# Attention and gated MLP on one core: the order of the first QKV tiles, two buffers and two kinds of adds changed

## The chip, the cores and the metric

The kernel runs on one core of a Trainium2 chip. The metric is the device time of one execution in microseconds (us); lower is better. The engines are named as the profile names them: PE (TensorE; PEld is its weight load), DVE (VectorE), ACT (ScalarE), POOL (GpSimd), SP (SyncE, which here only starts transfers). A name with a q (ACTq, POOLq, SPq) is the engine's DMA queue.

## The reference, cut to what matters

One layer in fp32 with S=2048 tokens and D=576 channels; the MLP has F=4608 hidden channels.

```python
q, k, v = heads_of(layernorm(x) @ wqkv)         # 32 heads of 18
# token s attends to s, s-2, ..., s-14 (W=8, dilation 2, none below 0)
logits = einsum("bhsd,bhswd->bhsw", q, kg) * Dh ** -0.5
o = einsum("bhsw,bhswd->bhsd", softmax(logits + mask), vg)
h = x + o @ wo
n = layernorm(h)
out = h + (sigmoid(n @ w_gate) * (n @ w_up)) @ w_down
```

## The kernel before, in words

**Tiles.** Tokens are split by parity (the dilation is 2) and by half into four blocks of 512 (`BLOCKS`, b = 0 to 3), each of four tiles of 128 (`NS`, index j). The 32 heads form four groups of eight (`NG`, index g).

**Products.** An fp32 product is made of three matmuls. `split` (L103 to L105) writes the high part with an ACT copy and the low part with a DVE subtraction; the products are high by high, low by high and high by low. So each operand of PE costs one pass of ACT and then one of DVE. The hidden size is cut into 36 pieces f of 128. For most of them two blocks are multiplied together by seven products of sums and differences instead of eight, and `sums` and `operands` make those sums.

**The attention stage**, the first 240 us or so:

- `ln1` (L327 on) norms a block. `ln_j` does one tile: statistics on DVE, a power on POOL, and then either DVE (L134, L135) or ACT (L130 to L132, with `on_act`) writes the normed tile. Before the change, ACT does it for blocks 2 and 3. PE transposes the tile (`tr_main`, L139, and `tr_rest`), and `split` makes `th` and `tl` of it.
- `qkv(b, g)` multiplies the four tiles of a block by the weights of one group (`tok_major`, L146 to L153). ACT evicts each product (L361). Behind the fourth eviction ACT's queue takes three transfers that write q (L363) and k and v (L366) to DRAM.
- `attention(b, g)` loads these rows through SP, multiplies and reduces them on DVE (L172, L175, L180 to L189, L198 to L206), with the softmax exponential on ACT (L185). For block 0 the result stays in SBUF; otherwise it is spilled to DRAM by POOL's queue (L209, L211).
- `att_all` holds the order of the attention work: (b, g) = (0,0), (0,1), (1,0), (0,2), (0,3), (1,1), (1,2), (1,3). It is interleaved by hand with the QKV work: `heads` runs `qkv` for a list of (b, g) and advances the attention by `step(ag, n)` after each tile, and `norm` does so between normed tiles. The groups of blocks 2 and 3 are attended later, under the MLP.
- `front` makes block 0's output projection, residual and second norm as soon as its four groups are attended.

**The MLP** runs over a list of pieces: 14 plain pieces for block 0 alone (`single`), 22 pieces for blocks 0 and 1 together (`pair`), 14 plain pieces for block 1 alone, and 36 pieces for blocks 2 and 3 together. Two pieces make a segment of the down product. In the plain pieces `down_std` makes a segment's four tiles (PE, L661) and adds them up in one SBUF tile called `stage`: the first of the seven segments by an ACT copy (L669), the other six by a DVE add (L671). Behind the seventh, `add_dram` (L677) adds the tile to DRAM through POOL's queue. The pool of `stage` tiles has two buffers. The pair segments go through ACT and `add_dram` in any case.

**Work under the MLP.** While PE multiplies, a background generator goes on with the rest: block 1's last attention, then for blocks 1 to 3 `proj_scr` (load of the spilled attention result `oj`, transposes, output projection, second norm), then `operands`, which makes the operands of the paired products. `proj_scr` copies its normed and transposed tiles to SBUF (`raw`) or, where `raw` is None, writes them tile by tile to DRAM (`xj`, `xscr`), from which `operands` loads them again as `ar`. Before the change, block 3 takes the way through DRAM: its operand sums (L260 to L270, in `sums`) wait for that load.

**The tail.** `load_tails` (L1021 to L1039) fetches the partial results of blocks 2 and 3 from DRAM into tiles `tail` and `more`, and three DVE adds (L1038) put them together under the last pieces. In the same pieces `pair` has three DVE adds of its own, L623, L636 and L641, which PE's next products wait for.

**What sets the order.** Each engine runs its instructions in a fixed order. A list scheduler writes that order from the program: it takes the ready instruction of the highest priority, `tc.high_priority(n)` raises the priority (HI = 400, HC = 700), and `tc.issue_after(x)` holds an instruction behind another one. A buffer of a pool is free again when its last reader is done.

Of the kernel before, what the change touches and what calls it, by code (L numbers as in the profile page):

```python
# [15 lines left out]
F32 = mybir.dt.float32  # L16
# [5 lines left out]
P = 128  # L22
S = 2048
D = 576
# [31 lines left out]
NPL = 4  # L56
LAG = 3


@with_exitstack  # L60
def kernel(ctx, tc, x, wqkv, wo, wmlp, out):
# [32 lines left out]
    hsev = dr.tile([P, 2, 7, 2, DH2], F32, name="h7")  # L94
    xscr = [dr.tile([P, 5, TB], F32, name=f"x{b}") for b in range(4)]
    wscr = [dr.tile([P, 2, 5, DH2], F32, name=f"wo{i}") for i in range(2)]
# [229 lines left out]
    def ln1(b, xb):  # L326
        th = th3_tile(F32R) if b == 3 else th_tile()  # L327
        tl = tl_tile()
        yield th, tl
        xn = tok_tile()  # L330
        for j in range(NS):
            js = slice(j * P, (j + 1) * P)
            pri = 2 * HI if b == 0 else HI if b > 1 else 0
            with tc.high_priority(pri):
                ln_j(xb[:, j], xn[:, j], b > 1)
            pv = tr_main(mm_tile(), xn[:, j])
            pr = tr_rest(acc_tile(), xn[:, j])
            with tc.high_priority(pri):
                split(th[:, 0:4, js], tl[:, :, js], pv)
                split_rest(th[:, 4, js], pr)  # L340
            yield
# [93 lines left out]
    wos = [None, wo_w(1, swo.tile([P, 2, 5, DH2], F32R, tag="wo", name="wo1"))]  # L435
    heads(((1, 2), (0, 3), (2, 2), (3, 2)), w, 2)
    wos[0] = wo_w(0, saw.tile([P, 2, 5, DH2], F32R, tag="qw", bufs=2, name="wow"))
# [151 lines left out]
    def single(X, w, t, units, side):  # L589
# [21 lines left out]
        return {t: hid}  # L611

    def pair(X, w, between, last):
        b1, b2, b3 = b_tile(0), b_tile(1), b_tile(2)
# [7 lines left out]
        with tc.high_priority(HC):  # L622
            dve.tensor_tensor(s1, s1, b2, ALU.add)  # L623
            act.activation(s1, s1, AF.Sigmoid)
# [9 lines left out]
        with tc.high_priority(HC):  # L634
            act.activation(s3, b1, AF.Copy)
            dve.tensor_tensor(s3, s3, b3, ALU.add)  # L636
        between(4)
        prod(b3, X["a11"], w, "t4", False)
        rest(b3, X["a11"], w, "g4")
        with tc.high_priority(HC):  # L640
            dve.tensor_tensor(s2, s2, b3, ALU.add)  # L641
            act.activation(s2, s2, AF.Sigmoid)
# [45 lines left out]
    def down_std(seg, b, n):  # L688
        if n == 0:
            tails[b] = st.tile([P, NS, D], F32, name="stage")  # L690
        hs = tails[b]
        for j in range(NS):
            add_tile(halved(hs, j), down_tile(seg, b, j), n == 0)
            if j == NS - 1 and n == NSTD // 2 - 1:
                add_dram(b, hs)
            yield
# [59 lines left out]
    def proj_scr(pj, b, raw, wos, ins=None, after=None):  # L756
# [3 lines left out]
        def tile_j(t, j):  # L760
            js = slice(j * P, (j + 1) * P)
            xj = []

            def put(pv, cs):
                if cs.start == 0:
                    if b < 2:
                        pool.dma_start(hacc[b][:, j], t[1])
                    else:
                        rows = slice(0, 7, 6) if b == 2 else slice(2, 5, 2)
                        pool.dma_start(hsev[:, j // 2, rows, j % 2],  # L770
                                       t[1].rearrange("p (i n) -> p i n", i=2))
                    if raw is None:
                        xj.append(pj.tile([P, 5, P], F32, bufs=2, name="xj"))
                act.activation(xj[0][:, cs] if raw is None else raw[:, cs, js], pv, AF.Copy)

            yield from proj_j(bg_bank, t, wos, th[:, :, js], tl[:, :, js], lambda: t[0], put, (1, 0))
            if raw is None:
                act.dma_start(xscr[b][:, :, js], xj[0])

# [25 lines left out]
        for j, gn in enumerate(live):  # L805
            yield from gn
            if after is not None:
                nxt.append([load_j(pj, after, j, i) for i in range(2)])
        if raw is not None:
            act.dma_start(xscr[b][:, 0:2], raw[:, 0:2])  # L810
        return nxt

    def operands(pp, p, Xn, names, own):
        def load(t):
            a = pp.tile([P, 5, TB], F32, name=f"ar{t}")
            pool.dma_start(a, xscr[2 * p + t])
            return a

        a0 = load(0) if p == 0 else own
        a1 = load(1) if p == 1 else own  # L820
        s = [pp.tile([P, 2, TB], F32, name=f"rs{i}") for i in range(3)]
# [14 lines left out]
    def under_first():  # L836
        wos = [None, wos_early()]
        for _ in ag:
            yield ATT
        at_stk.close()  # L840
        a1 = xt.tile([P, 5, TB], F32, tag="th", bufs=3, name="ar")
        with sb_pool("pj", "right") as pj:
            while c < 5:
                yield
            yield from proj_scr(pj, 1, a1, wos)
        with sb_pool("pp", "right") as pp:
            yield from operands(pp, 0, X, ("s2", "s3", "s1", "a11", "s4"), a1)

# [4 lines left out]
    def under_rest(last_x):  # L853
# [14 lines left out]
        with sb_pool("pj2", "right") as pj:  # L868
            a0 = xt.tile([P, 5, TB], F32, tag="th", bufs=3, name="ar")
            ins = yield from proj_scr(pj, 2, a0, wos, after=3)  # L870
            yield from proj_scr(pj, 3, None, wos, ins)
        z = st.tile([P, NS, D], F32, name="stage")
        pool.memset(z, 0.0)
        for u in range(2):
            act.dma_start(hsev[:, u, 1:6:2], z[:, 0:3].rearrange("p k (i n) -> p k i n", i=2))
        pp = pp_stk.enter_context(sb_pool("pp2", "right"))
        raw = yield from operands(pp, 1, Xn, ("s2", "s3", "s4"), a0)
        yield raw
# [142 lines left out]
    def load_tails():  # L1021
# [15 lines left out]
        for a, m in adds:  # L1037
            dve.tensor_tensor(a, a, m, ALU.add)  # L1038
            yield  # L1039
# [124 lines left out]
```

## Time and profile before

| | |
|---|---|
| time, three runs | 1611.44, 1617.32, 1623.48 us |
| median | 1617.32 us |
| profiled execution: time | 1618.58 us |
| profiled execution: span | 1616.8 us |
| mean granted PE clock in it | 0.991 |
| instructions in the span | 22443 |
| HBM read, written | 147.19 MB, 130.35 MB (172 GB/s over the span) |

The profile is one profiled execution, so its rows are to be set against its own 1618.58 us. On the page, part 1 gives the busy time of each engine with its share of the span; the parts after it are the span in 40 slices, the DMA queues, the chain of work that ended last, the costliest groups of instructions and the DMA issues. In a row for a group, "out<-in" are the tiles' names, "x4" the count, "3.0, 768" the busy time in us and the mean of one in ns, and what follows the last bar is the idle time of the engine ahead of them with the work that ended it. In a timeline a row begins with the start in us and the duration in us, and what stands in brackets at its end is the wait ahead of it. In a table of stretches each engine has its busy time and the number of its instructions, followed by the clock granted to PE.

### The profile page before, as it was taken

What the parts mean: (1) busy time and instruction counts of PE and PEld (TensorE: products, weight loads), DVE (VectorE), ACT (ScalarE), POOL (GpSimd) and SP (SyncE); (2) the same over time, 40 slices, a digit from 0 to 9 for tenths busy, and PEclk for the clock granted to TensorE, in tenths of its full rate; (3) what the DMA queues carried; (4) which work ended last, traced back from release to release, by engine and by line L of the source; (5) the groups of instructions that cost most, each with busy time, mean ns of one, the idle gap of its engine ahead of it and who ended that gap; (6) DMA issues with size and microseconds to landing.
All of it is one profiled execution on the core that took longest, in us unless ns stands there. A gap on an engine that the chain in (4) does not pass through costs nothing.

```text
span 1616.8 us, 22443 instructions
## 1 busy us (share of the span) xinstructions
PE 1570.3 (97%) x8532; PEld 1387.0 (86%) x8532; DVE 1277.2 (79%) x2002; ACT 877.2 (54%) x1537; POOL 184.8 (11%) x227
## 2 busy tenths in 40 slices
PE   7899889999999999999999999999999999999997
PEld 6899878887888888888898978888888888888887
DVE  7998898968999999999555668776677776677655
ACT  4423235434555566556434335776677776677651
POOL 2000010010001000000110100112112112112110
PEclk9999999999999999999999999999999999999999
DMA  7446555354367665675874435788888888888882
GB/s 246 177 149 225 216 180 183 113 196 173 103 161 192 167 152 154 157 197 141 252 230 153 136 109 150 154 167 181 171 169 189 174 168 181 169 172 189 170 185 94
DMA packets 79612, 276.65 MB, mean 171 GB/s; under 512 B 8368, under 2 KB 16816, under 8 KB 78480
## 3 DMA queue, kind: packets, MB, share of 16 engines
q0 software_dynamic: 28000, 107.79, 34.4%
q1 hardware_dynamic: 40304, 143.70, 27.3%
q10 hardware_dynamic: 11200, 23.73, 3.9%
q8 instruction: 67, 1.10, 0.3%
q14 instruction: 41, 0.34, 0.1%
HBM read 147.19 MB, written 130.35 MB: 172 GB/s over the span
## 4 chain that ended last, share of the span: by engine, by line
PE 64%; issue 17%; DVE 8%; DMA 6%; POOL 4%; ACT 1%; SPq 0%; POOLq 0%; ACTq 0%; DVEq 0%
PE b L554 30%; PE dp L661 13%; PE acc L150 6%; PE dp L723 6%; PE b L561 5%; POOL h L732 3%; DMA wg<-in_wmlp_dram 2%; DVE lg L175 1%; DVE w L105 1%; DVE pr L172 1%; DVE pr L198 1%; PE bgp L150 1%; PE b L150 1%; DMA o<-kw 1%; DMA kw<-k 1%
## 5 line engine op out<-in xcount | busy, mean ns | idle before, releaser
L554 PE MATMUL b<-tl,w 128*128 128x512 f32 x1728 | 446.6, 398 | 7.8 <-ACT s L628 4.1
L554 PEld LDWEIGHTS b<-tl,w 128*128 128x128 f32 x1728 | 313.8, 190 | 69.1 <-ACT s L628 5.4
L554 PE MATMUL b<-th,w 128*128 128x512 f32 x1380 | 359.6, 395 | 2.3 <-DVE s L574 2.3
L554 PEld LDWEIGHTS b<-th,w 128*128 128x128 f32 x1380 | 251.8, 189 | 56.4 <-DVE s L636 4.0
L561 PE MATMUL b<-th,w 128*128 128x512 f32 x576 | 178.0, 391 | 0.0
L104 ACT ACTIVATE w<-wg 128x384 fp32r<-128x384 f32 (+2 forms) x200 | 117.8, 595 | 106.8 <-DMA wg<-in_wmlp_dram 46.1
L729 ACT ACTIVATE ev<-dp 128x576 f32<-128x576 f32 x224 | 145.0, 648 | 33.2 <-PE dp L723 30.5
L732 POOL DMA_DIRECT2D h<-ev x128 | 109.8, 858 | 457.0 <-ACT ev L729 449.6
L105 DVE TENSOR_TENSOR w<-wg,w 128x384 fp32r<-128x384 f32 (+2 forms) x200 | 128.5, 648 | 39.0 <-ACT w L104 38.8
L150 PE MATMUL acc<-qw,th 128*128 128x432 f32 x512 | 156.8, 367 | 0.0
L105 DVE TENSOR_TENSOR w<-tw,w 128x512 fp32r<-128x512 f32 x116 | 79.6, 686 | 70.9 <-ACT w L104 70.3
L561 PEld LDWEIGHTS b<-th,w 128*128 128x128 f32 x576 | 108.6, 189 | 23.3
L661 PE MATMUL dp<-d,h1h 128*128 128x288 f32 x640 | 119.8, 296 | 2.4 <-ACT h1h L104 2.4
L104 ACT ACTIVATE w<-tw 128x512 fp32r<-128x512 f32 x116 | 73.3, 632 | 87.0 <-PE b L554 79.2
L661 PE MATMUL dp<-d,h0h 128*128 128x288 f32 x640 | 118.7, 295 | 1.0 <-ACT h0h L104 1.0
L661 PEld LDWEIGHTS dp<-d,h0h 128*128 128x128 f32 x640 | 99.6, 189 | 5.2 <-ACT h0h L104 1.2
L661 PEld LDWEIGHTS dp<-d,h1h 128*128 128x128 f32 x640 | 98.8, 189 | 5.6 <-ACT h1h L104 2.8
L150 PEld LDWEIGHTS acc<-qw,th 128*128 128x128 f32 x512 | 98.8, 193 | 4.8 <-ACT th L104 0.3
L150 PE MATMUL acc<-qw,tl 128*128 128x432 f32 x256 | 93.8, 367 | 0.0
L361 ACT ACTIVATE ev<-acc 128x432 f32<-128x432 f32 x64 | 33.9, 529 | 108.1 <-PE acc L153 107.7
L172 DVE TENSOR_TENSOR pr<-kw,q 128x1152 f32<-128x1152 f32 x64 | 85.2, 1353 | 7.9 <-DMA kw<-k 7.3
L669 ACT ACTIVATE stage<-dp 128x576 f32<-128x576 f32 x96 | 62.2, 648 | 53.3 <-PE dp L661 42.4
(270 smaller groups left out, 2898.8 us busy)
## 6 DMA issues: line engine op xcount, KB each, us to landing
h<-ev POOLq DMA_DIRECT2D x96, 576.0 KB, 6.8
wg<-in_wmlp_dram SPq DMA_DIRECT2D x49, 928.0 KB, 5.4
h<-stage POOLq DMA_DIRECT2D x24, 1152.0 KB, 11.7
wg<-in_wmlp_dram SPq DMA_DIRECT2D x36, 640.0 KB, 4.9
kw<-k SPq DMA_DIRECT2D x16, 792.0 KB, 4.7
vw<-v SPq DMA_DIRECT2D x16, 792.0 KB, 6.4
wd<-in_wmlp_dram SPq DMA_DIRECT2D x18, 576.0 KB, 6.7
h<-ev POOLq DMA_DIRECT2D x32, 288.0 KB, 6.1
```

What stands on the lines that cost most here:

```text
L104: act.activation(hi, src, AF.Copy)
L105: splits.append(dve.tensor_tensor(lo, src, f32(hi), ALU.subtract))
L150: pe.matmul(ps[:, :n], a[:, c, js], m[:, c], start=k == 0, stop=False)
L172: dve.tensor_tensor(pr[:, i], kw[:, j:j + W], q[:, j].unsqueeze(1).broadcast_to([P, W, CG]), ALU.mult)
L361: act.activation(ev[:, :, j], ps[:, :NQ].rearrange("p (t c) -> p t c", t=3), AF.Copy)
L554: pe.matmul(ps, wt[:, a, k0 + c], xx[:, m + c], start=first and k == 0, stop=k == 5, skip_group_check=True)
L561: pe.matmul(ps, wt[:, a, k0], xx[:, 4], start=False, stop=a == 1, skip_group_check=True)
L661: pe.matmul(ps[:, i, :DH2], a[:, js], d[:, m, i * DH2:(i + 1) * DH2], start=k == 0, stop=k == n)
L669: act.activation(hv, ps, AF.Copy)
L723: pe.matmul(ps[:, i, :DH2], a[x][:, js], m[y], start=k in (0, 1, 3) and q == 0, stop=q == 2, skip_group_check=True)
L729: act.activation(hs[:, k % 2], ps[:, :, :DH2], AF.Copy)
L732: pool.dma_start(hsev[:, u, k0:k + 1], hs[:, :k + 1 - k0], accum_op=ALU.add, max_dma_last_dim=8 * D)
```

## The change

Five things are changed.

1. The order of the QKV work: after the first two tiles of (1,2) come the four tiles of (0,3) and then the other two tiles of (1,2). Before, (0,3) came behind all four.
2. Block 1 is normed by ACT too (`b > 0` in `ln1`).
3. In the plain pieces of block 0, segments 0 to 4 (`NACC`) each start a new `stage` tile with ACT copies, and segments 0 to 3 and 6 are added to DRAM. So 16 DVE adds become ACT copies, and one DRAM add becomes five. Block 1's plain pieces stay as they were. Block 1's projection starts one piece later (`c < 6`).
4. Block 3's normed tiles are copied into an SBUF tile `ar3`, taken from the `stage` pool, and not written to DRAM and loaded again. Only two DRAM scratch tiles `xscr` are left. The zeroed `stage` tile and its two transfers move ahead of block 3's projection.
5. Each of the three tail adds is issued after the latest of `pair`'s own DVE adds (`added`).

```diff
@@ -55,6 +55,7 @@
 NSTD = 14
 NPL = 4
 LAG = 3
+NACC = (4, 0)
 
 
 @with_exitstack
@@ -92,7 +93,7 @@
     oscr = {b: dr.tile([P, NS, DX], F32, name=f"o{b}") for b in (1, 2, 3)}
     hacc = [dr.tile([P, NS, D], F32, name=f"h{b}") for b in range(2)]
     hsev = dr.tile([P, 2, 7, 2, DH2], F32, name="h7")
-    xscr = [dr.tile([P, 5, TB], F32, name=f"x{b}") for b in range(4)]
+    xscr = [dr.tile([P, 5 if b == 0 else 2, TB], F32, name=f"x{b}") for b in range(2)]
     wscr = [dr.tile([P, 2, 5, DH2], F32, name=f"wo{i}") for i in range(2)]
 
     def f32(ap):
@@ -332,7 +333,7 @@
             js = slice(j * P, (j + 1) * P)
             pri = 2 * HI if b == 0 else HI if b > 1 else 0
             with tc.high_priority(pri):
-                ln_j(xb[:, j], xn[:, j], b > 1)
+                ln_j(xb[:, j], xn[:, j], b > 0)
             pv = tr_main(mm_tile(), xn[:, j])
             pr = tr_rest(acc_tile(), xn[:, j])
             with tc.high_priority(pri):
@@ -433,7 +434,14 @@
     pads(3)
     h = load_x(0)
     wos = [None, wo_w(1, swo.tile([P, 2, 5, DH2], F32R, tag="wo", name="wo1"))]
-    heads(((1, 2), (0, 3), (2, 2), (3, 2)), w, 2)
+    first = qkv(1, 2, T[1], w[2])
+    for _ in range(2):
+        next(first)
+        step(ag, 2)
+    heads(((0, 3),), w, 2)
+    for _ in first:
+        step(ag, 2)
+    heads(((2, 2), (3, 2)), w, 2)
     wos[0] = wo_w(0, saw.tile([P, 2, 5, DH2], F32R, tag="qw", bufs=2, name="wow"))
 
     banks = [0]
@@ -610,6 +618,8 @@
         side(5)
         return {t: hid}
 
+    added = [None]
+
     def pair(X, w, between, last):
         b1, b2, b3 = b_tile(0), b_tile(1), b_tile(2)
         s1, s2, s3 = s_tile(), s_tile(), s_tile()
@@ -620,7 +630,7 @@
         prod(b2, X["a01"], w, "b10", True)
         rest(b2, X["a01"], w, "g4")
         with tc.high_priority(HC):
-            dve.tensor_tensor(s1, s1, b2, ALU.add)
+            added[0] = dve.tensor_tensor(s1, s1, b2, ALU.add)
             act.activation(s1, s1, AF.Sigmoid)
         between(1)
         prod(b1, X["s2"], w, "t2", False)
@@ -633,12 +643,12 @@
         rest(b1, X["a11"], w, "u4")
         with tc.high_priority(HC):
             act.activation(s3, b1, AF.Copy)
-            dve.tensor_tensor(s3, s3, b3, ALU.add)
+            added[0] = dve.tensor_tensor(s3, s3, b3, ALU.add)
         between(4)
         prod(b3, X["a11"], w, "t4", False)
         rest(b3, X["a11"], w, "g4")
         with tc.high_priority(HC):
-            dve.tensor_tensor(s2, s2, b3, ALU.add)
+            added[0] = dve.tensor_tensor(s2, s2, b3, ALU.add)
             act.activation(s2, s2, AF.Sigmoid)
         between(5)
         prod(b1, X["s4"], w, "b11", False)
@@ -686,12 +696,12 @@
 
 
     def down_std(seg, b, n):
-        if n == 0:
+        if n <= NACC[b]:
             tails[b] = st.tile([P, NS, D], F32, name="stage")
         hs = tails[b]
         for j in range(NS):
-            add_tile(halved(hs, j), down_tile(seg, b, j), n == 0)
-            if j == NS - 1 and n == NSTD // 2 - 1:
+            add_tile(halved(hs, j), down_tile(seg, b, j), n <= NACC[b])
+            if j == NS - 1 and (n < NACC[b] or n == NSTD // 2 - 1):
                 add_dram(b, hs)
             yield
 
@@ -759,7 +769,6 @@
 
         def tile_j(t, j):
             js = slice(j * P, (j + 1) * P)
-            xj = []
 
             def put(pv, cs):
                 if cs.start == 0:
@@ -769,13 +778,9 @@
                         rows = slice(0, 7, 6) if b == 2 else slice(2, 5, 2)
                         pool.dma_start(hsev[:, j // 2, rows, j % 2],
                                        t[1].rearrange("p (i n) -> p i n", i=2))
-                    if raw is None:
-                        xj.append(pj.tile([P, 5, P], F32, bufs=2, name="xj"))
-                act.activation(xj[0][:, cs] if raw is None else raw[:, cs, js], pv, AF.Copy)
+                act.activation(raw[:, cs, js], pv, AF.Copy)
 
             yield from proj_j(bg_bank, t, wos, th[:, :, js], tl[:, :, js], lambda: t[0], put, (1, 0))
-            if raw is None:
-                act.dma_start(xscr[b][:, :, js], xj[0])
 
         todo = []
         if ins is None:
@@ -806,18 +811,14 @@
             yield from gn
             if after is not None:
                 nxt.append([load_j(pj, after, j, i) for i in range(2)])
-        if raw is not None:
-            act.dma_start(xscr[b][:, 0:2], raw[:, 0:2])
+        if b == 1:
+            act.dma_start(xscr[b], raw[:, 0:2])
         return nxt
 
-    def operands(pp, p, Xn, names, own):
-        def load(t):
-            a = pp.tile([P, 5, TB], F32, name=f"ar{t}")
-            pool.dma_start(a, xscr[2 * p + t])
-            return a
-
-        a0 = load(0) if p == 0 else own
-        a1 = load(1) if p == 1 else own
+    def operands(pp, p, Xn, names, a0, a1):
+        if p == 0:
+            a0 = pp.tile([P, 5, TB], F32, name="ar0")
+            pool.dma_start(a0, xscr[0])
         s = [pp.tile([P, 2, TB], F32, name=f"rs{i}") for i in range(3)]
         rd = pp.tile([P, TB], F32, name="rd")
         if p == 1:
@@ -840,11 +841,11 @@
         at_stk.close()
         a1 = xt.tile([P, 5, TB], F32, tag="th", bufs=3, name="ar")
         with sb_pool("pj", "right") as pj:
-            while c < 5:
+            while c < 6:
                 yield
             yield from proj_scr(pj, 1, a1, wos)
         with sb_pool("pp", "right") as pp:
-            yield from operands(pp, 0, X, ("s2", "s3", "s1", "a11", "s4"), a1)
+            yield from operands(pp, 0, X, ("s2", "s3", "s1", "a11", "s4"), None, a1)
 
     Xn = {}
     pp_stk = ExitStack()
@@ -868,13 +869,15 @@
         with sb_pool("pj2", "right") as pj:
             a0 = xt.tile([P, 5, TB], F32, tag="th", bufs=3, name="ar")
             ins = yield from proj_scr(pj, 2, a0, wos, after=3)
-            yield from proj_scr(pj, 3, None, wos, ins)
-        z = st.tile([P, NS, D], F32, name="stage")
-        pool.memset(z, 0.0)
-        for u in range(2):
-            act.dma_start(hsev[:, u, 1:6:2], z[:, 0:3].rearrange("p k (i n) -> p k i n", i=2))
+            z = st.tile([P, NS, D], F32, name="stage")
+            pool.memset(z, 0.0)
+            for u in range(2):
+                act.dma_start(hsev[:, u, 1:6:2],
+                              z[:, 0:3].rearrange("p k (i n) -> p k i n", i=2))
+            ar = st.tile([P, 5, TB], F32, tag="stage", name="ar3")
+            yield from proj_scr(pj, 3, ar, wos, ins)
         pp = pp_stk.enter_context(sb_pool("pp2", "right"))
-        raw = yield from operands(pp, 1, Xn, ("s2", "s3", "s4"), a0)
+        raw = yield from operands(pp, 1, Xn, ("s2", "s3", "s4"), a0, ar)
         yield raw
 
     phase = None
@@ -1035,7 +1038,8 @@
                     adds.append((hs[:, h], h2))
         yield from lag(7)
         for a, m in adds:
-            dve.tensor_tensor(a, a, m, ALU.add)
+            with tc.issue_after(getattr(added[0], "ins", added[0])):
+                dve.tensor_tensor(a, a, m, ALU.add)
             yield
 
     def twice(i):
```

## The prediction

> **What bounds the kernel now.** I read the page's busy shares first, then the waits of TensorE (PE), then a table of stretches around the longest waits, and last the timelines of ScalarE (ACT) and VectorE (DVE) inside them.
>
> ```profile
> PE 1570.3 (97%) x8532; PEld 1387.0 (86%) x8532; DVE 1277.2 (79%) x2002; ACT 877.2 (54%) x1537; POOL 184.8 (11%) x227
> core 0: us, PE busy (x) PEld busy (x) DVE busy (x) ACT busy (x) POOL busy (x), PEclk, DMA share, GB/s
> 65.00:79.00 14.00, 9.97 (x42) 8.18 (x41) 13.48 (x19) 8.55 (x21) 0.00 (x0) 0.76 0.32 121
> 187.00:198.00 11.00, 6.25 (x28) 5.37 (x27) 9.69 (x19) 2.71 (x8) 0.00 (x0) 0.69 0.88 317
> 236.00:246.00 10.00, 6.26 (x20) 4.22 (x19) 9.94 (x10) 5.16 (x8) 0.00 (x0) 0.83 1.04 398
> 324.00:331.00 7.00, 4.04 (x19) 3.27 (x18) 3.34 (x5) 1.74 (x5) 0.00 (x0) 0.76 0.79 281
> 380.00:406.00 26.00, 22.21 (x108) 18.54 (x107) 22.34 (x36) 10.67 (x19) 0.00 (x0) 0.93 0.58 213
> 933.00:943.00 10.00, 6.57 (x26) 5.27 (x25) 8.19 (x9) 4.28 (x6) 0.00 (x0) 0.83 0.28 95
> 1575.00:1584.00 9.00, 4.91 (x20) 3.94 (x19) 4.58 (x4) 1.42 (x3) 0.00 (x0) 0.81 0.57 211
> ```
>
> PE is the bound, and no edit removes a matmul; what can be won are PE's idle times and the halved clock behind them. In each stretch the idle time is its length less PE's busy time, and the clock's loss is its length times (1 - PEclk). In order that gives 4.0+3.4, 4.75+3.4, 3.7+1.7, 3.0+1.7, 3.8+1.8, 3.4+1.7 and 4.1+1.7 us: 42 us in seven places. Between them PE runs through. But in the first 320 us DVE is nearly full as well, so an idle time taken from PE there comes back if DVE is not earlier too.
>
> **Block 1 normed by ScalarE.**
>
> ```profile
> L130 ACT ACTIVATE tok<-h,nm 128x576 f32<-128x576 f32 x4 | 3.0, 768 | 2.6 <-DVE nm L129 2.6
> L131 ACT ACTIVATE tok<-tok,rstd 128x576 f32<-128x576 f32 x4 | 3.0, 767 | 0.5 <-POOL rstd L126 0.5
> L134 DVE TENSOR_SCALAR tok<-h,mv,rstd 128x576 f32<-128x576 f32 x4 | 2.3, 576 | 1.1 <-POOL rstd L126 1.1
> 28.36 0.43 ACTq L366 DMA_DIRECT2D k<-ev  x1
> 35.03 1.36 DVE L172 TENSOR_TENSOR pr<-kw,q 128x1152 f32<-128x1152 f32 x1 [1.89 <-DMA kw<-k]
> 36.98 0.51 ACT L361 ACTIVATE ev<-acc 128x432 f32<-128x432 f32 x1
> 45.61 2.55 DVE L175 TENSOR_REDUCE lg<-pr 128x128 f32<-128x2304 f32 x1
> 53.90 0.69 DVE L105 TENSOR_TENSOR tl<-mm,th 128x512 fp32r<-128x512 f32 x1
> 57.25 0.69 DVE L105 TENSOR_TENSOR tl<-mm,th 128x512 fp32r<-128x512 f32 x1
> 58.53 0.42 DVE L184 TENSOR_TENSOR lg<-lg,mx 128x256 f32<-128x256 f32 x1
> 58.99 0.42 ACT L185 ACTIVATE lg<-lg 128x256 f32<-128x256 f32 x1 [0.59 <-DVE lg L184]
> 52.67 0.60 ACT L104 ACTIVATE th<-mm 128x512 fp32r<-128x512 f32 x1
> 53.70 0.44 PE L150 MATMUL acc<-qw,th 128*128 128x432 f32 x1
> 67.34 1.10 PE L139 MATMUL mm<-ident,tok 128*128 128x128 f32 x6 [1.28 <-ACT tok L131]
> ```
>
> Four tiles take 4 x 1.5 us on ACT and save 4 x 0.58 us of DVE (the 64-column copies move too). By itself that lies under QKV matmuls. The order does not: in the changed program ACT issues the k rows of block 0's first group after the 7th eviction (L361) instead of the 4th, for six norm passes and three evictions now stand before it. The 7th ends at 37.5, with two small copies the issue comes at about 37.8 instead of 28.36, 9.4 us later, so the first attention product (L172) starts at 35.03 + 9.4 = 44.4. Before the reduce (L175) DVE then has two products and two split pairs, 4.7 us: 49.1 instead of 45.61, DVE 3.5 us late.
>
> Next in line: the changed order has the softmax exponential (L185) ahead of the 12th eviction and of block 2's splits (L104, th) on ACT, and the softmax ahead of the tl splits on DVE; before, both came behind them. From L175 to the end of L184 took 13.3 us, of which the splits (53.90 to 57.9) were 4.0, so the end falls at 49.1 + 9.3 = 58.4. Exponential, eviction and split add 1.5: th is there at 59.9 instead of 53.27, and PE waits for it. That is 6.6 us; I add 1.7 for one halved stretch as in the table: +8.3. Bounds: 0, if k lands in time after all, and 6.6 + 3.4 = +10. I take the upper half, since the wait for k and the order of both queues are there in rows; the loss has no cover, PE has nothing else queued.
>
> The same edit puts block 3's first two normed tiles one eviction sooner: the 1.28 and 0.3 us gaps at 66 to 69 go, -1.6 (to -7.4 if that stretch closes). PE is then 6.7 us late.
>
> **Block 0's last group two tiles sooner.**
>
> ```profile
> 150.31 0.53 ACT L361 ACTIVATE ev<-acc 128x432 f32<-128x432 f32 x1 [2.22 <-PE acc L153]
> 154.00 0.45 ACTq L366 DMA_DIRECT2D k<-ev  x1
> 163.48 2.63 DVE L172 TENSOR_TENSOR pr<-kw,q 128x1152 f32<-128x1152 f32 x2 [5.42 <-DMA kw<-k]
> 190.89 0.46 DVE L206 TENSOR_TENSOR tok<-pr 128x288 f32<-128x288 f32 x1
> ```
>
> DVE stood 5.42 us for these k rows, and PE's idle time at 187 to 198 waits for the end of that attention. The changed order issues them after the 43rd eviction, not the 44th: 2.8 us sooner, not two tiles. With PE 6.7 us late that is 3.9 us later than before; DVE (3.5 late, with 5.4 of slack) is not what decides. The attention ends at 195.3, PE, which began to wait at 187, comes at about 193.7 and waits some 1.6: 8.2 us of that stretch go, 6.7 + 1.6 come, net about 0 at 198 (bounds +4 and -9.8, the latter without the exponential's wait). DVE is about 4 us late there. At 236 to 246 PE waits for DVE's first weight splits; half of DVE's lateness is made up in its small waits on PE, so +2 (0 to +4).
>
> **Four plain segments added in DRAM.**
>
> ```profile
> L671 DVE TENSOR_TENSOR stage<-stage,dp x9: 740/746/748, 282.5 to 318.7; 128x576 f32<-128x576 f32 x9
> L669 ACT ACTIVATE stage<-dp 128x576 f32<-128x576 f32 x96 | 62.2, 648 | 53.3 <-PE dp L661 42.4
> h<-stage POOLq DMA_DIRECT2D x24, 1152.0 KB, 11.7
> 319.08 0.71 POOL L209 DMA_DIRECT2D o<-kw  x1 [41.75 <-DVE kw L206]
> 327.74 1.12 PE L139 MATMUL b<-ident,oj 128*128 128x128 f32 x4 [2.96 <-DMA oj<-o]
> ```
>
> 16 adds of 0.75 us leave DVE and 16 copies of 0.65 us come to ACT; 9 of the adds lay before 319, 6.7 us. Block 1's last attention ends by so much sooner, less DVE's lateness over PE, so about 5; but the changed order also puts the oj transposes 26 matmuls sooner, at PE's mean of 1570.3/8532 = 0.18 us a time of 4.8 us. The spill and the load behind it stay 8.7 us (319.08 to 327.74), so a wait like the 2.96 stays. So 0 (-3 to +2). A down tile comes every (318.7 - 282.5)/8 = 4.5 us, four make a transfer, so the new ones of 11.7 us lie 18 us apart on the Pool queue; the last spill stands behind the second of them, which is due at about 297, some 20 us before it: 0, and up to +2 if they slow the oj loads. The stretch 380 to 406 has 7 adds fewer, but the operand sums come one segment later, nearer to the pair stage that needs them: I take -1.5 of its 5.6 (0 to -5.6).
>
> **Block 3's result kept in SBUF; tail adds tied.**
>
> ```profile
> 921.07 0.52 ACTq L778 DMA_DIRECT2D x<-xj  x1
> 933.83 1.23 DVE L262 TENSOR_TENSOR rs<-ar 128x1024 f32<-128x1024 f32 x1 [3.92 <-DMA ar<-x]
> 935.69 0.63 ACT L104 ACTIVATE h1h<-s 128x512 fp32r<-128x512 f32 x1 [5.14 <-DVE s L574]
> 1576.84 1.36 DVE L1038 TENSOR_TENSOR tail<-tail,more 128x1152 f32<-128x1152 f32 x1 [4.43 <-DMA tail<-h]
> 1578.11 0.68 DVE L623 TENSOR_TENSOR s<-s,b 128x512 f32<-128x512 f32 x1
> 1578.83 0.63 ACT L624 ACTIVATE s<-s 128x512 f32<-128x512 f32 x1 [5.66 <-DVE s L623]
> 1579.99 2.92 PE L554 MATMUL b<-tl,w 128*128 128x512 f32 x6 [4.09 <-ACT s L628]
> ```
>
> At 933 DVE stood behind the first operand sum, which waited for the round trip through DRAM from 921; the segment's hidden product, its split and PE stood behind DVE. ACT now writes the operand where it is used: all of the 5.1 us go (bounds -3.4, if only the idle time goes, and -5.1). The zeroed stage tile moves ahead of block 3's projections and its slot is needed only at their end, so I cost that at nothing; late, it would bring the old wait back. At 1576 the first tail add waited for its load ahead of L623. Tied, it stands behind L623: PE's 5.8 go. The second add then stands ahead of the last gate sum (L641) and may cost half of its 1.36: -5.1 (-4 to -5.8).
>
> **Sum.** 0 + 2 + 0 - 1.5 - 5.1 - 5.1 = -9.7 on the profiled execution's 1618.58 us (span 1616.8 and 1.8 around it): 1608.9. That execution lies 1.3 us over the median of the three runs, 1617.32, so I say 1608.
>
> The table halves the clock after waits of 3.0 us and of 2.4 + 1.0 us. [...]
>
> **Rivals.** (1) The exponential holds nothing up: its input comes in time, or PE loses only what it would have waited at 187. For it: DVE has 5.42 us of slack at 158. Against it: k's issue is held by evictions that PE itself times. Then +8.3 falls away, PE waits at neither 66 nor 187, DVE is not late at 236: front -1.6 - 8.2 instead of +2, 11.8 less: 1596; with the whole of the stretch at 380, 1592. (2) Slower: ACT, in order, blocks the new copies.
>
> ```profile
> 367.33 0.74 ACT L104 ACTIVATE w<-wg 128x640 fp32r<-128x640 f32 x1 [5.60 <-DMA wg<-in_wmlp_dram]
> ```
>
> ACT stands up to 5.6 us for a weight load, and a down tile comes every 4.5 us with two buffers. From a hold of some 8 us PE stands for the copy; 2 us at each of 16 makes +32 and 1640. Against it: before, the first segment's copies ran with no wait of PE for them. (3) The tied adds only pass the wait on (to L636 and L641), no gain there: 1613.
>
> **How the numbers follow.** A measurement of this kernel can tell about 1%, 16 us: faster means under 1601, slower over 1633. Forecast 0.42 and rival 3 0.06 are both within: 0.48. Rival 1 has 0.40: one arrival, 6 us sooner, decides it, and three later waits hang on it. Rival 2 and other waits at new places, 0.12. Rival 1's 1592 less 2 for the spread of the runs sets the low end; the high end is the forecast with the upper bounds at 198, at 236 and of the transfers (4 + 2 + 2) and rival 3's 5: 1621.
>
> **What would show it.** Right: k issued near 38 and ACT's first exponential near 58.5 with PE idle 5 to 7 us before it; no DVE wait for ar, no PE wait near 934 and 1576; the wait for oj still 2 to 3 us. Wrong: PE running through 53 to 61; no idle time at 187 with PE early; PE waiting for L669 in the plain segments.

## The result, and the profile after

The changed kernel took 1633.58 us, median of six runs (1630.70 to 1638.93), against 1618.41 for the kernel before (six runs): ratio 1.0100, 95% interval 1.0068 to 1.0132. The forecast was 1608 with a range up to 1621. The profiled execution is the shortest of the six, 1630.70 us with a span of 1628.5, which is 11.7 us more than the span before.

The first row of part 1 of the page, and a table of stretches: the seven of the prediction, then the places where PE waits now. After the length come the busy times of PE, PEld, DVE, ACT and POOL, each with its count, then the clock granted to PE.

```profile
PE 1573.4 (97%) x8532; PEld 1387.9 (85%) x8532; DVE 1265.6 (78%) x1982; ACT 888.6 (55%) x1565; POOL 188.9 (12%) x230
```

```profile
38.00:46.00 8.00, 4.62 (x24) 3.87 (x23) 5.30 (x21) 5.57 (x14) 1.65 (x3) 0.81 1.02 348
57.00:65.00 8.00, 2.87 (x17) 2.36 (x16) 7.22 (x11) 3.05 (x10) 0.00 (x0) 0.90 0.49 175
65.00:79.00 14.00, 12.71 (x65) 11.84 (x64) 13.22 (x17) 8.01 (x17) 0.00 (x0) 0.93 0.28 100
79.00:88.00 9.00, 6.75 (x24) 5.61 (x25) 8.68 (x11) 3.37 (x9) 0.00 (x0) 0.62 0.26 98
187.00:198.00 11.00, 10.90 (x64) 10.21 (x62) 10.86 (x19) 3.35 (x8) 0.00 (x0) 1.00 0.67 206
236.00:246.00 10.00, 7.06 (x31) 5.56 (x30) 9.90 (x10) 3.61 (x7) 1.32 (x2) 0.92 0.98 365
300.00:310.00 10.00, 7.18 (x29) 5.76 (x28) 8.53 (x12) 6.48 (x10) 1.20 (x1) 0.83 0.80 177
328.00:346.00 18.00, 11.09 (x51) 8.95 (x49) 5.26 (x10) 5.56 (x11) 0.00 (x0) 0.72 1.00 325
380.00:406.00 26.00, 26.00 (x149) 23.03 (x148) 21.59 (x30) 15.48 (x26) 0.58 (x1) 1.00 0.44 145
786.00:794.00 8.00, 4.72 (x30) 4.19 (x29) 4.03 (x6) 2.93 (x5) 0.00 (x0) 1.00 1.02 371
820.00:832.00 12.00, 5.50 (x28) 4.94 (x27) 2.92 (x5) 3.32 (x7) 0.67 (x1) 0.72 1.02 397
933.00:943.00 10.00, 10.00 (x66) 9.13 (x65) 5.15 (x8) 4.46 (x10) 0.00 (x0) 1.00 0.27 97
1575.00:1584.00 9.00, 9.00 (x46) 7.36 (x45) 3.65 (x6) 4.52 (x8) 1.73 (x2) 1.00 0.93 207
```

Read as in the prediction (length less PE's busy time, and length times 1 - clock), the old waits at 187, 380, 933 and 1575 are gone. The stretch of 65 to 79 now lies some 9 us later and is hardly shorter (2.3 + 3.4 at 79 to 88, and 1.3 + 1.0 ahead of it), and the wait for `oj` has grown from 3.0 + 1.7 at 324 to 331 to 6.9 + 5.0 at 328 to 346. New are 3.4 + 1.5 us at 38 to 46, 5.1 + 0.8 at 57 to 65, 2.8 + 1.7 at 300 to 310, 3.3 at 786 and 6.5 + 3.4 at 820.

PE has the same 8532 matmuls in every profile here, so its lag can be followed: the start of the n-th matmul less the start of the n-th in the kernel before, for n = 850, 1000, 1260, 1800, 2000, 3900, 4300, 5000, 8200 and 8520. The table gives what the lag gained between these points, in us; the head gives the times of the points in the kernel before. Each row is one profiled execution, and the first column scatters by 1 to 4 us with block 1 on DVE (e2, e5, e6, e11, e12); so the times of the experiments are judged by their medians, and the rows tell the place.

| us | to 183 | to 212 | to 270 | to 367 | to 411 | to 757 | to 825 | to 947 | to 1550 | to 1611 | sum |
|---|---|---|---|---|---|---|---|---|---|---|---|
| forecast | +6.7 | -6.7 | +2 | 0 | -1.5 | 0 | 0 | -5.1 | 0 | -5.1 | -9.7 |
| the change | +10.0 | -5.8 | -0.2 | +9.9 | -6.2 | +1.0 | +11.5 | -5.6 | +2.0 | -4.5 | +12.2 |
| e1 start at c < 5 | +11.1 | -5.8 | +1.1 | +10.0 | -2.4 | +0.9 | -0.3 | -5.7 | +1.6 | -4.5 | +6.1 |
| e2 block 1 on DVE | +3.7 | -4.6 | +0.9 | +6.8 | -6.1 | +0.6 | +14.8 | -6.1 | +6.2 | -4.5 | +11.6 |
| e3 one SBUF sum | +11.4 | -5.6 | -0.3 | -0.2 | -5.9 | +0.7 | +11.4 | -5.1 | +2.4 | -4.4 | +4.4 |
| e4 both e1 and e3 | +14.0 | -5.6 | -0.4 | +1.7 | -1.6 | 0.0 | 0.0 | -5.9 | +2.7 | -4.5 | +0.2 |
| e5 order, SBUF, tied | +1.3 | -0.1 | +2.1 | -2.6 | -1.6 | 0.0 | 0.0 | -4.8 | +1.9 | -4.5 | -8.3 |
| e6 SBUF, tied | +1.9 | -1.7 | +0.3 | +0.4 | -0.1 | 0.0 | 0.0 | -5.5 | +3.7 | -4.5 | -5.5 |
| e8 copies, no adds | +9.8 | -5.0 | +0.2 | -3.1 | -5.9 | +1.0 | +12.9 | -5.9 | +2.9 | -3.7 | +3.2 |
| e11 e5, c < 6 | +1.4 | -0.9 | +0.2 | -3.7 | -6.0 | +0.7 | +14.9 | -5.5 | +1.3 | -4.5 | -2.1 |
| e12 e11, no pause | +2.5 | -4.7 | +2.7 | -3.9 | -6.0 | +2.2 | -0.3 | -5.7 | +1.5 | -4.5 | -16.0 |

Three places make the loss: up to 183 us, 270 to 367, and 757 to 825.

### The profile page after: what moved, and what is told of

It is laid out like the page before. It is cut to its first block, busy times and chain, and to the rows that moved or that the text cites. A ratio compares the mean times of both kernels' runs of the same rounds, so it can differ in the third digit from the quotient of the medians.

```text
span 1628.5 us, 22454 instructions
## 1 busy us (share of the span) xinstructions
PE 1573.4 (97%) x8532; PEld 1387.9 (85%) x8532; DVE 1265.6 (78%) x1982; ACT 888.6 (55%) x1565; POOL 188.9 (12%) x230
## 4 chain that ended last, share of the span: by engine, by line
PE 77%; DVE 10%; DMA 8%; issue 2%; ACT 2%; SPq 0%; POOL 0%; ACTq 0%; DVEq 0%; POOLq 0%
PE b L562 39%; PE dp L671 13%; PE dp L733 11%; PE b L569 7%; DMA wg<-in_wmlp_dram 3%; PE acc L151 3%; DVE pr L173 2%; DVE pr L199 2%; DVE lg L176 1%; DMA o<-kw 1%; PE bgp L151 1%; PE b L151 1%; DVE w L106 1%; DMA oj<-o 1%; DMA kw<-k 1%
## 5 line engine op out<-in xcount | busy, mean ns | idle before, releaser
L679 ACT ACTIVATE stage<-dp 128x576 f32<-128x576 f32 x112 | 72.0, 645 | 53.9 <-PE dp L671 42.6
```

The lines of the kernel that those rows point to most:

```text
L679: act.activation(hv, ps, AF.Copy)
```

## The experiments

My theory from these rows was that each of the three has a cause of its own: block 1 on ACT, the traffic of the DRAM adds, and the start of block 1's projection at `c < 6`. The rival was one cause with several effects, PE's lag from the front meeting later loads.

| kernel | median, us | ratio to before, 95% interval |
|---|---|---|
| the change | 1633.58 | 1.0100 (1.0068 to 1.0132) |
| e1 change, start at c < 5 | 1627.23 | 1.0062 (1.0038 to 1.0085) |
| e2 change, block 1 on DVE | 1624.38 | 1.0054 (1.0031 to 1.0077) |
| e3 change, one SBUF sum | 1622.24 | 1.0036 (1.0016 to 1.0055) |
| e4 change, e1 and e3 | 1615.21 | 0.9991 (0.9974 to 1.0009) |
| e5 before + order, SBUF, tied | 1607.31 | 0.9931 (0.9914 to 0.9948) |
| e6 before + SBUF, tied | 1608.91 | 0.9949 (0.9930 to 0.9967) |
| e7 e4, block 1 first on ACT | 1612.72 | 0.9966 (0.9953 to 0.9979) |
| e8 change, no DRAM adds | 1621.01 | 1.0024 (1.0010 to 1.0037) |
| e9 e4, q, k, v issued first | 1611.35 | 0.9969 (0.9956 to 0.9982) |
| e10 e4, e7 and e9 | 1615.21 | 0.9982 (0.9969 to 0.9995) |
| e11 e5, start at c < 6 | 1615.41 | 0.9985 (0.9972 to 0.9998) |
| e12 e11, no pause | 1603.41 | 0.9917 (0.9896 to 0.9937) |
| e13 e7, first k issued first | 1612.26 | 0.9971 (0.9955 to 0.9987) |
| e14 e12, block 1 as in e13 | 1608.06 | 0.9950 (0.9932 to 0.9967) |

The ratios are to runs of the kernel before on the same chip (medians 1616.6 to 1618.4).

**The parts taken back.** e1, to the change:

```diff
-            while c < 6:
+            while c < 5:
```

> The whole change, but block 1's projection starts one piece earlier again (c < 5 as before). Theory A (the start sets DVE's order): block 3's last attention ends one piece earlier, before the 57th hidden product; its spill is written some 20 us earlier, the oj loads find it, the weight load behind them on SP's queue isn't held, and PE's waits at 789 (3.3 us) and 822 (6.5 us) with their halved clock go: 10 to 13 us faster than the change, about 1621. Theory B (the DRAM adds or PE's own lag hold the spill and the loads): the late waits stay, within 3 us of the change, 1631 to 1636.

e2, to the change:

```diff
-                ln_j(xb[:, j], xn[:, j], b > 0)
+                ln_j(xb[:, j], xn[:, j], b > 1)
```

> The whole change, but block 1 is normed by DVE again. Theory A (ACT's order in the first 80 us costs PE 9.3 us, of which the wait at 187 gives 5.8 back): PE runs through 39 to 44 and 58 to 64, waits at 66 to 72 as before, and waits some 3 to 4 us again at 187: 3 to 6 us faster than the change, 1628 to 1631. Theory B (the front's delay goes through to the end in full, since the QKV order alone closes the wait at 187): 9 us faster, about 1624. Theory C: the front is made up for elsewhere and the time is that of the change.

e3, to the change (e4 has this and the edit of e1):

```diff
-NACC = (4, 0)
+NACC = (0, 0)
```

> The whole change, but block 0's plain segments are added up in one SBUF tile again (NACC = (0, 0)); the projection starts at c < 6. Theory A (the DRAM adds slow the transfers beside them, so the oj load took 11.4 us to land where it took 4.1): oj lands in about 4 to 5 us, PE waits there 2 to 4 us instead of 6.9 with 5.1 of halved clock, and the waits at 302 (2.8 us) go: 6 to 10 us faster than the change, 1624 to 1628. Theory B (oj is late because block 1's attention is, and PE's order wants it 26 matmuls sooner): the wait stays at 6 us or more, within 3 us of the change.

> Both at once: one SBUF sum and the start at c < 5; left of the change are the QKV order, block 1 on ACT, block 3 in SBUF and the tied adds. Theory A: the two gains add up, 16 to 21 us faster than the change, 1613 to 1618, less up to 6 us if the waits at 380 to 406 come back. Theory B: 0 to 5 us faster.

e1 came 6.4 us below the change, less than expected: the +11.5 before 825 is gone as foreseen, but 3.8 of the 6.2 us won at 367 to 411 went with it. e2 gave 9.2 us, what theory B said; its profiled execution was a long one (span 1628.3), so its row in the table shows less of that gain. e3 gave 11.3 us, more than expected, and its row has it at 270 to 367. e4 gave 18.4: the two add up. With this the rival of one cause falls: e1 and e3 each take away the loss of one place and leave the others, and e2, whose row has no lag left at 270 us, still loses 6.8 us from 270 to 367 and 14.8 from 757 to 825.

**What is left.** e5 is the kernel before with parts 1, 4 and 5 of the change, and e6 with parts 4 and 5; their edits are those of the diff.

> The kernel before with three parts of the change: the QKV order, block 3 in SBUF and the tied adds; block 1 on DVE, one SBUF sum, start at c < 5. Theory A (from the runs so far: block 1 on ACT costs 9 us to the end, the other two left out cost 6 to 11 us each): about 9 us faster than the version that differs from it only in block 1's norm (1615.2): 1604 to 1608, and PE's waits at 187 to 198 and 236 to 246 are shorter by some 9 us than before. Theory B (the front's waits only move: what block 1 on ACT costs at 40 to 80 is what PE waits for at 187 to 246 otherwise): 1612 to 1616.

> The kernel before with only block 3 in SBUF and the tied adds. Theory A (the waits at 934 and 1576 go, 5.1 us each, less a new wait of 1 to 2 us near 1000): 8 to 10 us faster than before, 1607 to 1610; then the QKV order is worth the rest of the step to the version with it, 2 to 5 us. Theory B (the waits pass on to the pair's own sums): 0 to 4 us, 1613 to 1617.

Both times lie in theory A's ranges: parts 4 and 5 win 8.9 us (1617.86 to 1608.91 on that chip), and block 1 on ACT costs 7.9 (e4 less e5). The QKV order's 1.6 is less than the 2 to 5 expected, and the intervals of e5 and e6 overlap, so it isn't clear of the noise. Nor are the waits of e5 at 187 to 198 and 236 to 246 shorter by 9 us, but by 5.5 in its profile (4.3 + 2.5 and 1.2, where 4.8 + 3.4 and 3.7 + 1.7 stood), and its row shows no gain up to 270. The steps -8.9 - 1.6 + 7.9 + 18.4 = +15.8 lead from the kernel before to the change one by one, so they must give the measured 15.2 but for the difference between chips; the sum shares the loss out and is no check of it.

**The DRAM adds.** e8, to the change:

```diff
-            if j == NS - 1 and (n < NACC[b] or n == NSTD // 2 - 1):
+            if j == NS - 1 and n == NSTD // 2 - 1:
```

> The whole change with the same ACT copies into new tiles in block 0's plain segments, but the four extra transfers that add them to DRAM are left out, so segments 0 to 3 are missing from the result. Theory A (the traffic is what costs): oj lands in 4 to 5 us, the oj wait is 2.5 to 4 us as with one SBUF sum (3.6 measured), PE's waits at 240 to 310 but for those at 241 and 244 go, and the time is within 3 us of 1622.2. Theory B (the copies on ACT and the new place of the oj products cost): the oj wait stays above 5.5 us and the time at 1630 or more.

It ran in 1621.0 us, theory A's time; `oj` landed in 5.9 us, not 4 to 5, and PE's wait for it fell to 1.3. The DMA issues and the transfer rate from 310 to 345 us (40 slices), first the change, then e8:

```profile
GB/s 399 17 0 0 0 0 119 161 416 382 27 0 0 0 0 0 216 210 120 110 246 331 331 229 242 243 238 259 232 243 255 349 416 478 421 421 421 379 406 400
...
oj<-o SPq DMA_DIRECT2D x4, 320.0 KB, 11.4
h<-stage POOLq DMA_DIRECT2D x1, 1152.0 KB, 12.7
```

```profile
GB/s 0 51 136 399 441 59 19 0 0 0 0 169 229 140 102 280 339 403 364 401 416 439 487 434 403 369 385 390 350 311 407 314 42 36 0 0 0 0 0 0
...
oj<-o SPq DMA_DIRECT2D x4, 320.0 KB, 5.9
```

While the third add runs, all transfers together move 229 to 259 GB/s by the profile's count (330 to 337 us), against 350 to 487 in e8 (325 to 335), and the oj load takes 11.4 us to land, not 5.9. The third add stands right behind the spill on POOL's queue in the change:

```profile
300.62 1.20 POOL L687 DMA_DIRECT2D h<-stage  x1 [17.86 <-ACT stage L679]
322.99 0.75 POOL L210 DMA_DIRECT2D o<-kw  x1 [21.16 <-DVE kw L207]
323.65 0.84 POOL L212 DMA_DIRECT2D o<-kw  x1
325.42 1.22 POOL L687 DMA_DIRECT2D h<-stage  x1 [0.92 <-ACT stage L679]
```

PE's waits for oj and for ACT, of the change and then of e8, in the waits between 280 and 420 us (total, times, longest):

```profile
PE b L140 <- DMA oj<-o: 6.2, 1, 6.2
PE dp L671 <- ACT h0h L105: 2.1, 1, 2.1
```

```profile
PE b L140 <- DMA oj<-o: 1.3, 1, 1.3
```

The wait for ACT begins further ahead. Behind the first add, issued at 281.5, ACT stood 5.20 us for a weight load in the change, and 1.32 in e8:

```profile
292.65 1.15 ACT L105 ACTIVATE w<-wg 128x640 fp32r<-128x640 f32 x2 [5.20 <-DMA wg<-in_wmlp_dram]
```

No cost of the copies on ACT shows: at 270 to 367 the row of e8 gains 2.9 us on that of e3 (-3.1 against -0.2), though their medians are only 1.2 us apart, which the intervals don't separate. The adds then take 13.0 us in the rows (+9.9 against -3.1) and 12.6 by the medians. e8 takes them away as a whole; that they cost by slowing the loads is read from the landing times. A `stage` tile held by its add is not the reason, since ACT's copies waited for PE alone from 236 to 420 us (5.3 us in 7 waits).

**The start one piece later.** e11, to e5, and e12, to e11:

```diff
-            while c < 5:
+            while c < 6:
```

> The version with the QKV order, block 3 in SBUF and the tied adds (1607.3), with block 1's projection started one piece later (c < 6) and nothing else. Theory A (the start alone moves block 3's last attention one piece later): the waits at 380 to 416 go (up to 3 us and a halved clock here), the two waits near 780 and 815 come with 10 to 12 us: 5 to 8 us slower, 1612 to 1616. Theory B (it takes the DRAM adds or block 1 on ACT as well): within 2 us of 1607.3.

```diff
-        skip = () if kind == "std" else (3,)
+        skip = ()
```

> The same start at c < 6, but the attention of blocks 2 and 3 isn't held back at one of the seven places of each pair (skip = ()), which puts block 3's last attention back ahead of the 57th hidden product. Theory A: the spill comes as early as before, SP's queue isn't held by the oj loads, the waits near 780 and 815 are gone while those at 380 to 416 stay away: 1600 to 1605, faster than every version so far. Theory B (the loads are late for another reason, such as the transfer that writes block 0's output): the waits near 780 and 815 stay, 1612 to 1616.

e11 is 8.1 us slower than e5, just above what was expected, and e12 is 12.0 us faster than e11: theory A in both times. The queues of SP and POOL and ACT's longest wait in e11, and the first two in e12:

```profile
786.88 14.15 SPq L522 DMA_DIRECT2D oj<-o  x3
801.14 0.85 SPq L515 DMA_DIRECT2D wg<-in_wmlp_dram  x1
```

```profile
786.49 1.18 POOL L686 DMA_DIRECT2D h<-stage  x1 [23.53 <-ACT stage L678]
788.47 0.78 POOL L209 DMA_DIRECT2D o<-kw  x1 [0.80 <-DVE kw L206]
```

```profile
812.65 0.74 ACT L104 ACTIVATE w<-wg 128x640 fp32r<-128x640 f32 x1 [10.86 <-DMA wg<-in_wmlp_dram]
```

```profile
781.41 1.87 SPq L522 DMA_DIRECT2D oj<-o  x3
790.53 0.33 SPq L515 DMA_DIRECT2D wg<-in_wmlp_dram  x1
```

```profile
772.46 0.75 POOL L209 DMA_DIRECT2D o<-kw  x1 [7.61 <-DVE kw L206]
```

In e11 block 3's last attention result is spilled at 788.5, after SP has begun with the oj loads that need it. They take 14.15 us to issue, the next weight load stands behind them until 801, and ACT stands 10.9 us for it; PE's 6.0 us wait follows. In e12 the spill is out at 772.5, the loads issue in 1.87 us, and PE runs through 760 to 830 (busy for 70.00 of the 70 us). In the changed kernel the same rows lie some 15 us later:

```profile
802.44 14.44 SPq L523 DMA_DIRECT2D oj<-o  x3
816.99 0.70 SPq L516 DMA_DIRECT2D wg<-in_wmlp_dram  x1
```

The spill goes out only 1.6 us after the first oj load; the rest of the 14 us is its landing (11.1 us). In e11 the spill was issued 2.0 us behind the add of a pair segment on POOL's queue (786.49) and took 11.3 us to land; in e5 it was issued 5.7 us ahead of that add and took 4.6. The other wait that comes with the later start, PE's 3.3 us at 786 to 794 in the change, has the same form. The load `tw` (part of an operand, fetched again under the last pair piece of blocks 0 and 1) was issued 1.2 us behind the add of the segment before; ACT stood 5.0 us for it, DVE stood 4.9 behind ACT, and PE waited the 3.3 us for a DVE sum. The rows of the change:

```profile
778.74 1.20 POOL L687 DMA_DIRECT2D h<-stage  x1 [16.33 <-ACT stage L679]
779.96 0.33 SPq L933 DMA_DIRECT2D tw<-x  x1
788.51 1.06 ACT L105 ACTIVATE tl<-tw 128x1024 fp32r<-128x1024 f32 x1 [5.03 <-DMA tw<-x]
```

```profile
tw<-x SPq DMA_DIRECT2D x1, 512.0 KB, 8.5
o<-kw POOLq DMA_DIRECT2D x1, 288.0 KB, 11.1
```

All 16 profiles divide in this way. In the five with both waits (the change, e2, e3, e8, e11) the spill is 2.0 to 2.6 us behind an add and lands in 11.0 to 11.4 us, and `tw` 1.2 us behind one and lands in 8.5 to 8.8. In the other eleven the spill is 5.7 us or more ahead of that add and lands in 4.1 to 6.6 us, and `tw` 3.1 us or more ahead and lands in 3.4 to 3.5. No run takes these adds away, so that they are what slows the two transfers is read from the rows and not shown by an edit.

**Block 1 on ACT.** Four kernels tried to make it free. e7, to e4:

```diff
-            pri = 2 * HI if b == 0 else HI if b > 1 else 0
+            pri = 2 * HI if b < 2 else HI
```

> The version with the QKV order, block 1 on ACT, block 3 in SBUF and the tied adds, but block 1's norm and splits get a priority above block 2's, so that ACT norms block 1's last two tiles before block 2's and has the splits of block 2 ahead of the exponential; k of block 0's first group is still issued after the 7th eviction. Theory A (the two places in ACT's order are the price, not ACT's work): PE runs through at 39 to 44 and at 58 to 64, 8 to 10 us faster than with the old priorities (1615.2), about 1606. Theory B (k's late issue is the price, since DVE then is late instead): the waits come back as PE waits for DVE at 66 to 80 or at 187 to 198, and the time stays at 1612 to 1616.

e9, to e4 (e10 has both edits, and e13 has both with the priority for (b, g) = (0, 0) alone):

```diff
+        with tc.high_priority(2 * HI):
             act.dma_start(qscr[b][g], ...)
...
                 act.dma_start(s[e][g][r0:r0 + TB, :]...
```

> The version with the QKV order, block 1 on ACT, block 3 in SBUF and the tied adds (1615.2), but the transfers that write q, k and v get a high priority, so that k of block 0's first group is issued after the 4th eviction again, near 28 us; block 1's last two tiles are still normed behind block 2's, and the exponential still stands ahead of the splits. Theory A (k's late issue makes DVE late, and that is the wait at 54 to 64): the first attention product starts near 36 instead of 46.8, the wait before block 2's first QKV tile falls from 4.8 us to under 1, PE's lag at its 600th matmul falls from 13 to some 5 us (the wait at 39 to 44 stays), and the time is 3 to 8 us shorter, 1607 to 1612. Theory B (the order on ACT holds PE, whenever k comes): the wait stays over 4 us, 1613 to 1617.

> The same with both: q, k and v issued at once, and block 1's norm and splits ahead of block 2's. Theory A: neither the wait at 39 to 44 nor the one at 53 to 64 is left, PE's lag at its 600th matmul is at most 2 us, and block 1 on ACT costs nothing: 1605 to 1609, the time of the version with block 1 on DVE (1607.3). Theory B (ACT's own six us more of work is the price): 1611 to 1615.

> As the run with both priorities (1615.2), but only the transfers of block 0's first group have the high priority, so that ACT doesn't stand 6.4 us at the issue of the second group's v, as it did there at 39 to 45 ahead of block 1's splits. Block 1's norm stands ahead of block 2's, and the exponential behind block 2's splits. Theory A (the places in ACT's order and k's issue are the whole price of block 1 on ACT): no wait of PE over 2 us from 38 to 66, a lag of at most 3 us at the 600th matmul, 1605 to 1609, as with block 1 on DVE (1607.3). Theory B (ACT's six us more of work is a price in any order): a wait of 4 us or more comes at some place before 70, 1611 to 1615.

PE's waits of over 1.5 us up to 66 us, as the timelines of PE give them, in e4, e7, e9 and e13 in turn:

```profile
42.21 0.66 PE L139 MATMUL mm<-ident,tok 128*128 128x128 f32 x4 [2.68 <-ACT tok L131]
44.95 1.09 PE L139 MATMUL mm<-ident,tok 128*128 128x128 f32 x4 [1.60 <-DVE mv L124]
64.95 0.66 PE L150 MATMUL acc<-qw,th 128*128 128x432 f32 x1 [4.83 <-ACT th L104]
```

```profile
59.56 1.12 PE L139 MATMUL mm<-ident,tok 128*128 128x128 f32 x4 [6.13 <-DVE tl L105]
```

```profile
41.24 0.66 PE L139 MATMUL mm<-ident,tok 128*128 128x128 f32 x4 [3.02 <-ACT tok L131]
46.37 1.09 PE L139 MATMUL mm<-ident,tok 128*128 128x128 f32 x4 [3.85 <-DVE rstd L125]
```

```profile
44.29 1.12 PE L139 MATMUL mm<-ident,tok 128*128 128x128 f32 x4 [4.56 <-DVE tl L105]
```

e4 has both waits: block 1's last two tiles, whose norm stands behind block 2's on ACT, and block 2's splits behind the exponential. e7 mends both places in ACT's order, and the wait comes back as DVE's lateness, as theory B said, while k is still issued late. e9 issues k at 27.1 us and of the second wait 1.2 us are left, 3.9 us faster; the first stays and grows, from 4.3 to 6.9 us in all. e10 doesn't tell, since ACT stood 6.4 us at the issue of the second group's v there. e13 takes that away and still has 4.56 us (in a profile that is the longest of its twelve runs, 1616.9 us): k was issued at 27.9, but SP now issued block 2's x and weights beside it, the load of k went out at 35.2, not 30.3 as in e5, and DVE stood 5.4 us for it. So A's numbers failed in e10 and e13, and B's 1611 to 1615 hold (e10's 1615.2 at their end). e14 puts e13's edits into e12:

> The fastest version so far (QKV order, block 3 in SBUF, tied adds, start at c < 6, no pause in the attention: 1603.4) with block 1 on ACT in that order. Theory A: the time stays within 2 us of 1603.4, or falls by up to 3 if DVE's six us less show at 187 to 250. Theory B: 1607 to 1611.

It is 4.7 us slower than e12, B again. Each order cost 4 to 9 us. Whether some order is free, or ACT's added work always costs, is open. So is where all of it is paid: the rows put 4.0 us (the change less e2) and 4.7 (e4 less e5) of lag at 270 us, of 9.2 and 7.9 in the medians.

## Why the prediction was wrong, point by point

- **Block 1 on ACT, +6.7 at 187: right in mechanism, too small.** k was issued at 35.6 (37.8 foreseen), the first attention product started at 46.8 (44.4), since the load of k went out at 41.4, and the exponential ran at 61.1 (58.5). PE's waits for the splits behind it were 4.28 and 0.84 us, with 1.8 us of lost clock: 6.9 where 6.6 + 1.7 = 8.3 stood. What failed is "By itself that lies under QKV matmuls": block 1's norm has no priority (0) and block 2's has, on an engine that they now share, so PE waited 2.59 and 0.64 us for block 1's own last tiles, with 1.5 us of lost clock. Nor did the -1.6 for block 3's first tiles come: PE's waits for them were 3.9 us before and are 3.5 now, at 79 to 84, with the clock's loss unchanged at 3.4 us. The rows of the changed kernel, ACT's and PE's:

```profile
35.63 0.36 ACTq L367 DMA_DIRECT2D k<-ev  x1
...
40.71 0.79 ACT L132 ACTIVATE tok<-tok,rstd 128x576 f32<-128x576 f32 x1
...
61.10 0.42 ACT L186 ACTIVATE lg<-lg 128x256 f32<-128x256 f32 x1 [6.83 <-DVE lg L185]
```

```profile
41.55 0.66 PE L140 MATMUL mm<-ident,tok 128*128 128x128 f32 x4 [2.59 <-ACT tok L132]
...
62.47 0.46 PE L151 MATMUL acc<-qw,th 128*128 128x432 f32 x1 [4.28 <-ACT th L105]
```

- **The stretch at 187 and the one at 236:** the step of -6.7 measured -5.8, and +2 measured -0.2. Together with the 3.3 us too little before, the front ended 4 us late, where 2 was foreseen.
- **The DRAM adds, 0 (-3 to +2): wrong, +9.9.** Two parts of this term were right: DVE is earlier without the 16 adds (2.9 us in e8's row), and the second add came at 300.6 (297 foreseen), ahead of the spill. The step that failed is "0, and up to +2 if they slow the oj loads": I placed the second add and not the third, which came 0.9 us after the spill's last issue and ran beside the oj loads, and priced the sharing at 2 us at most; all four adds cost 13 us. The profile of before had a row for that price: its oj loads landed in 4.1 us at 324 with no add beside them, and in 8.9 at 788, 0.4 us behind an add.
- **380 to 406, -1.5: the gain was -6.2,** its upper bound and a little more. It came from the later start, not from DVE's relief: e11 has it (-6.0) with one SBUF sum, and e1, without the start, has -2.4. Of the kernels with the old start only e7 has it as well (-5.6); why is open.
- **`c < 6` had no price of its own: +11.5 before 825.** The prediction priced the later start only for the operand sums of blocks 0 and 1. The attention of blocks 2 and 3 is queued behind those sums (`under_rest` is issued after the last split), so its end moved a piece later: its spill and the load `tw` came behind adds to DRAM that they had been ahead of, and the oj loads that wait for the spill held a weight load on SP's queue. None of this was followed, 400 us on.
- **Block 3 in SBUF, -5.1:** measured -5.6, with a new wait near 1004, for `pair`'s second DVE add, that I hadn't foreseen (+2.0 up to 1550, and in e6 too). **Tail adds, -5.1:** measured -4.5. These two steps held.
- **The rivals.** ACT blocking on the new copies (1640) has the right sign and the wrong mechanism; e8 has the copies and not the loss at 270 to 367. That the exponential holds nothing up, and that the tied adds pass the wait on, both fell. What came about lies in "other waits at new places", for which the prediction had a share of 0.12 and no time.
- **The clock.** The prediction put a halved clock behind a wait, as the table of before shows it (0.76 over the 7 us at 324, 0.83 over the 10 us at 933; 1.7 us of loss each). In the change not every wait had it: a single wait of 3.3 us at 786 to 794 left the clock at 1.00, but 2.8 us of idle time at 300 to 310, in two waits of 2.1 and 0.7, left it at 0.83 (0.50 from 306 to 309). What decides between the two is not shown. At 933 the row held: taking the wait away brought 5.6 us, more than its 3.4 us of idle time.

## What to carry to other kernels

An edit that only moves a start moves everything that is queued behind it: follow it to the last transfer that depends on it, and see what stands behind that transfer on its queue and what runs beside it. Here the price of a DRAM add of 1152 KB was set not by its own landing time (12.7 us) but by the loads beside it (11.4 us to land, not 5.9). The version that is faster than both kernels (e12, 1603.4 us) keeps the parts that take a wait away and leaves the ones that load a second engine or the DMA queues.

## What the runs showed of the hardware that I had not expected

Beside a transfer that adds to DRAM, the sum of all transfers fell to 229 to 259 GB/s (the change, 330 to 337 us), from 350 to 487 in the same stretch without it (e8, 325 to 335), and loads of 320 KB took 11.4 us where they took 5.9. Beside the adds of the pair segments a spill of 288 KB took 11.1 us and a load of 512 KB 8.5 (the change), where they took 4.7 and 3.4 ahead of such adds (the kernel before). One load on SP's queue that waits for its data held the weight load behind it for 14.4 us (the change) and 14.2 (e11).
